# Later ranks of a mixture-of-experts layer get a PSUM bank of their own, and queued sums move to later blocks

## The chip, the cores and the metric

The kernel runs on one core of one Trainium2 chip. The metric is the time of one execution on the device in microseconds (us); the number shown for a kernel is the median of its runs.

## What is computed

Three parts follow one another. Pooled attention (8 batches, 8 heads, 576 positions, head size 64; keys and values averaged over groups of 8) gives 4608 tokens of width 512. Two mixture-of-experts layers follow, each with 8 experts and one expert per token:

```python
    logits = x @ w_gate + modality_bias[modality_id]
    e_idx = np.argmax(logits, axis=1)
...
        h = np.maximum(x[mask] @ w1[e], 0.0)
        out[mask] = gate_w[mask, None] * (h @ w2[e])
```

The second layer has no bias, and it computes only tokens with `x @ w_skip > 0`; a token it skips passes through, and a token it computes is added to its result:

```python
    do_compute = skip_score > 0
    out = x.copy()
    xc = x[do_compute]
...
    out[do_compute] = xc + y
```

The weights are `w1` (8 x 512 x 1024) and `w2` (8 x 1024 x 512), all in fp32.

## The kernel before, in words

Tokens are sorted by expert into blocks of 256. Every fp32 product is made of three products of a high and a low half (`xh`, `xl`, `w1h`, `w1l` and so on). Layer 1 has 18 static blocks, numbered 0 to 17 here, and `body1(i, end)` emits block i:

- **gemm1**: eight steps f, each 12 matmuls of 128x256. Two steps share a PSUM bank (tag "g1", three banks); after the second of a pair ACT writes `hh` (L1474) and DVE `hl` (L1475). Pair 3 (f = 6, 7) reuses the bank of pair 0.
- **gemm2(i, 0)**: 24 matmuls of 128x512, three for each of eight places f. The dictionary `at` hangs work on places. At f = 2 and 4 `next_x` transposes the next block's rows on PE into PSUM (tag "tp", two banks); ACT writes `xh` (L1420) and DVE `xl` (L1423) from there.
- **gemm2(i, 1)**: the other 128 rows, 24 matmuls.

While block i is multiplied, the second layer's routing is made for block i - 1's rows. For each block a queue `todo` holds 18 sums (`logit`, L1800, on DVE), then the two halves of `picks`: `first` (POOL L1731 to L1741, with `rt_mx` on DVE, L1738) and `second` (`rt_my` on DVE, L1747; then POOL `M` L1750, `carry` L1752, `rti` L1753, and the scatter of rows). `drip(n)` takes from the queue until n sums or picks are done. `rank(i)` is two small matmuls on PE (L1779, L1780) into the bank `R2`, a chain of five operations on DVE up to `BB` (L1784 to L1788), and on POOL `RH` (L1789) and four one-hot matrices `OB` (L915). So the chain of one block's routing is: 18 sums, `rt_mx`, POOL's `first` up to `rt_eq`, `rt_my`, POOL's `M`, `carry`, `rti`, then PE's rank, `BB`, `OB`. Each engine works in the order in which its instructions are written.

`arms` holds for blocks 6 to 13, `armed` for blocks 7 to 14. In armed blocks DVE splits the weights of a new expert if there is one, in place of sums; what stayed in the queue is made up in gemm2. Armed blocks rank at place 6 of gemm2(i, 0), the others inside gemm1 after f = 4 and 6:

```python
            if f in (4, 6) and ranks and not armed:
                m.rank(ranks.pop(0))
...
            at = {0: m.drip, 5: pick, 6: partial(m.rank_all, ranks)}
...
            m.drip(8 if armed else 7)
```

In block 16 the second layer's blocks begin to be planned ahead: `start2` has ACT cast the carries (`rc_cb`, L932), and PE sums them over partitions (L936) after f = 1 of gemm1 into the bank of tag "m" (one bank). In block 17 (`late`) the first rows of layer 2 are gathered (POOL L1336, DVE `gi` L1637). After gemm2(17, 0) the head of the queue is taken out as `second`, three sums are dripped, block 18's rows are transposed, and then what was taken out is done:

```python
            _, _, second = m.todo.pop(0)
            m.drip(3)
            next_x(0)
            next_x(1)
            second()
```

Of the kernel before, what the change touches and what calls it, by code (L numbers as in the profile page):

```python
# [9 lines left out]
F32 = mybir.dt.float32  # L10
# [14 lines left out]
E = 8  # L25
# [804 lines left out]
def route(tc, g, r, lg, mask, c0, n, sp, pp, eng, wait=1, then=(), lag=(0, 0)):  # L830
# [52 lines left out]
    for _ in range(4 if wait else 1):  # L883
        yield
    R = pp.tile([128, n, E], F32, tag="m", name="R")
    nc.tensor.matmul(R, lhsT=g.trim, rhs=M, start=True, stop=False)
    nc.tensor.matmul(R, lhsT=g.ones, rhs=I, start=False, stop=True)
    g.bg.hold = True
# [5 lines left out]
    B = r.BB[:, c0:c0 + n]  # L894
    V.tensor_tensor(rk, M, R, ALU.mult)
    yield
# [12 lines left out]
def route_places(tc, g, r, c0, n, eng, eng2=None):  # L909
    for c in range(c0, c0 + n):  # L910
        for i in range(2):
            if c > c0:
                yield
            e = eng2 if eng2 is not None and i else eng
            e.tensor_scalar(g.ob(c)[:, i, :], g.iota, r.BB[:, c:c + 1],  # L915
                            r.pay[:, i, c:c + 1], ALU.is_equal, ALU.mult)
        yield
# [10 lines left out]
def count(tc, g, r, sp, pp, wait, copy=False, cb=None):  # L928
    nc = tc.nc
    if cb is None:  # L930
        cb = sp.tile([128, E], BF16, tag="rc_cb", name="rc_cb", bufs=1)
        (nc.scalar.copy if copy else nc.vector.tensor_copy)(cb, r.carry)  # L932
        for _ in range(wait):
            yield
    N = pp.tile([128, E], F32, tag="m", name="R")
    nc.tensor.matmul(N, lhsT=g.ones, rhs=cb, start=True, stop=True)  # L936
# [256 lines left out]
class Moe:  # L1193
# [575 lines left out]
            in_=self.x2[i % 2][:, t, 0:DM], in_offset=None, bounds_check=NT - 1,  # L1769
            oob_is_err=False)  # L1770

    def rank(self, i):

        nc, g, r2 = self.nc, self.g, self.g.r2
        V = nc.vector
        M, I = r2.M[:, 2 * i:2 * i + 2, :], self.rti[i % 2]
        B = r2.BB[:, 2 * i:2 * i + 2]
        R = self.ps_t("R2")[:, 0, 0:2 * E].rearrange("p (c e) -> p c e", e=E)
        nc.tensor.matmul(R, lhsT=g.trim, rhs=M, start=True, stop=False)  # L1779
        nc.tensor.matmul(R, lhsT=g.ones, rhs=I, start=False, stop=True)  # L1780
        rk = self.sp.tile([128, 2, E], F32, tag="rt_rk", name="rt_rk")
        ra = self.sp.tile([128, 2], F32, tag="rt_ra", name="rt_ra")
        ri = self.sp.tile([128, 2], I32, tag="rt_ri", name="rt_ri")
        V.tensor_tensor(rk, M, R, ALU.mult)  # L1784
        V.tensor_reduce(out=ra, in_=rk, axis=AX.X, op=ALU.add)
        V.tensor_copy(ri, ra)
        V.tensor_scalar(ri, ri, 127, None, ALU.bitwise_and)
        V.tensor_copy(B, ri)  # L1788
        nc.gpsimd.tensor_tensor(r2.RH[:, 2 * i:2 * i + 2], ra, B, ALU.subtract)  # L1789
        for _ in route_places(self.tc, g, r2, 2 * i, 2, nc.gpsimd):  # L1790
            pass

    def rank_all(self, ranks=None):
        ranks = self.ranks if ranks is None else ranks
        while ranks:
            self.rank(ranks.pop(0))

    def logit(self, i, t, e):

# [29 lines left out]
class Layer:  # L1829
# [28 lines left out]
    def second(self):  # L1858

        m, g = self.m, self.m.g  # L1860
        bg = g.bg
        for f in range(8):
            m.gemm1(1, f)
            bg.tick()
            bg.tick()
        m.gemm2(1, 0, self.epilogue)
        bg.flush()
        self.gather(2)
        self.gather(3)
        self.load_regs(2)  # L1870
        self.load_w1(2)
        self.load_w2(2)
        m.load_split(2)
        m.split_w1_if(range(8))
        m.drip(7)
        m.gemm2(1, 1, self.epilogue, {3: lambda: m.xT(2, 0, m.ps_t("ps_x")),
                                      5: lambda: m.xT(2, 1, m.ps_t("ps_x")),
                                      6: lambda: m.gates1(2, m.sp)})
        m.gates2(2, m.sp)
        m.drip(5)  # L1880
# [85 lines left out]
    def body1(self, i, end):  # L1966

        m = self.m
        late = i == self.n_static - 1
        arms = self.ARMS <= i < self.n_static - 4  # L1970
        armed = self.ARMS <= i - 1 < self.n_static - 4
        ranks = m.ranks
        m.ranks = []
        for f in range(8):
            m.gemm1(i, f)
            if f in (1, 3):
                if armed:
                    m.sums_or_w2(f)
                else:
                    m.split_w2_if(range(2 * f - 2, 2 * f + 2))  # L1980
            m.drip(((0, 0, 1, 0, 1, 0, 1, 1) if armed else
                    (0, 0, 1, 1, 1, 1, 2, 2) if late else (1, 1, 1, 2, 1, 2, 1, 1))[f])
            m.g.bg.tick()
            if f in (4, 6) and ranks and not armed:
                m.rank(ranks.pop(0))
            if f == 5 and i == self.n_static - 2:
                m.places2()
            if f == 6 and late:
                m.gather2(i + 1)
                m.load_w1_parts(2, m.e2, end, range(4))  # L1990
        if not armed:
            m.rank_all(ranks)
        m.g.bg.flush()
        m.g.bg.pace = 2
        full = self.load_full(i)
        more = i + 1 < NBLK or end is not None
        if i + 1 < NBLK:
            self.load_w2(i + 1)
        if end is not None:
            m.load_w2_parts(2, m.e2, end)  # L2000

        def next_x(t):
            if t == 0 and end is not None:
                m.gates1(i + 1, m.sp)
            m.xT(i + 1, t, m.ps_t("ps_x"))
            if t == 1:
                m.gates2(i + 1, m.sp)

        if armed:
            new = m.load_split_dve(i)  # L2010

            def pick():
                m.settle_sums()
                m.sums_left(new)
                m.drip()

        if more:
            m.load_split(i + 1)
            if end is None:
                m.gates1(i + 1, m.sp)  # L2020
            m.split_w1_if(range(4))
        if armed:
            at = {0: m.drip, 5: pick, 6: partial(m.rank_all, ranks)}
        elif end is None:
            at = {f: m.drip for f in ((0, 1, 5, 6) if i > 8 else (0, 1, 3, 5, 6))}
        elif late:
            at = {f: m.drip for f in (0, 1, 3, 5)}
        else:
            n = sum(x[1] for x in m.todo) - 2
            at = {f: partial(m.drip, (n + j) // 5) for j, f in enumerate((0, 1, 3, 5, 6))}  # L2030
            at[7] = m.drip
        if more and not late:
            at.update({2: lambda: next_x(0), 4: lambda: next_x(1)})
        m.gemm2(i, 0, self.epilogue, at)
        if late:
# [5 lines that stand above are left out]
        if arms:  # L2041
            m.sums_or_w1(i, range(4, 8))
        elif more:
            m.split_w1_if(range(4, 8))
        if arms:
            pass
        elif end is None:
            m.drip(8 if armed else 7)
        elif not late:
            m.drip()  # L2050
        with m.tc.If(full > 0):
            m.gemm2(i, 1, self.epilogue)
# [126 lines left out]
```

## Time and profile before

| what | us |
|---|---|
| median of 3 runs (lowest, highest) | 932.89 (929.35, 934.34) |
| the profiled execution's own time | 931.96 |
| its span in the profile | 929.9 |
| PE busy | 887.1 (95%) |
| DVE busy | 706.9 (76%) |
| POOL busy | 505.9 (54%) |
| ACT busy | 370.7 (40%) |

The profile is one execution of the program. PE is TensorE, PEld its weight loads, DVE VectorE, ACT ScalarE, POOL GpSimd, SP the engine that issues most DMAs. A row of a timeline gives the start in us from the span's start, the duration, the engine, the source line, the operation with output and inputs, and in brackets how long the engine was idle before and which instruction ended that. Times of all rows are on the clock of the execution before. PEclk is the share of full clock that TensorE was granted.

### The profile page before, as it was taken

Reading aid. Unit: us, or ns where it says so; the run is one execution under the profiler, and the core shown is the slowest. Engines: PE = TensorE matmul, PEld = TensorE weight load, DVE = VectorE, ACT = ScalarE, POOL = GpSimd, SP = SyncE. Lnnn points to the kernel's source line nnn. Section 1 sums busy time; section 2 is a strip of 40 time slices with the busy share of each in tenths; the row PEclk is TensorE's granted clock in tenths of the full one; section 3 lists DMA queues with packets and bytes.
Section 4 is the critical chain, followed back from the end, with each engine's and each line's share of the span. In section 5 each row is a group of like instructions: output and inputs, shape, how many; then the busy total and the mean of one; then the engine's idle time right before and its main releaser. Section 6 shows DMA issues by size and latency. Waiting matters only on the chain. (4 is left out here: it accounts for less than half of the span.)

```text
span 929.9 us, 19087 instructions
## 1 busy us (share of the span) xinstructions
PE 887.1 (95%) x6233; PEld 797.1 (86%) x6233; DVE 706.9 (76%) x1828; ACT 370.7 (40%) x738; POOL 505.9 (54%) x758
## 2 busy tenths in 40 slices
PE   8999999889999999999999978999999999999995
PEld 6899889879899999988888867899888988979983
DVE  5687888877778888789877888877666778687772
ACT  4666556552222222252222511213314566565551
POOL 5796783322346656575766657575652444445441
PEclk9999999999999999999999998999999999999997
DMA  9999954423311221612225321236215772761441
GB/s 233 241 285 294 274 154 147 164 82 111 97 59 65 71 66 40 222 65 68 87 82 185 120 79 65 76 104 227 70 61 166 218 257 88 222 221 36 134 142 44
DMA packets 85950, 126.08 MB, mean 136 GB/s; under 512 B 13000, under 2 KB 49912, under 8 KB 85674
## 3 DMA queue, kind: packets, MB, share of 16 engines
q1 hardware_dynamic: 75194, 96.68, 34.0%
q0 software_dynamic: 10608, 27.67, 9.9%
q8 instruction: 63, 1.03, 0.5%
q14 instruction: 85, 0.70, 0.2%
HBM read 182.09 MB, written 39.50 MB: 238 GB/s over the span
## 5 line engine op out<-in xcount | busy, mean ns | idle before, releaser
L1470 PE MATMUL ps_g<-xh,w1h 128*128 128x256 f32 x896 | 256.8, 287 | 2.2 <-DVE o L1709 1.3
L1470 PE MATMUL ps_g<-xl,w1h 128*128 128x256 f32 x896 | 253.8, 283 | 0.7 <-DVE xl L1423 0.7
L1470 PE MATMUL ps_g<-xh,w1l 128*128 128x256 f32 x896 | 252.8, 282 | 0.0
L1800 DVE CUSTOM_DVE_ANT_0 hr<-x,W 128x512 bf16<-128x512 f32 x324 | 227.8, 703 | 15.7 <-DVEq L1399 4.9
L1519 PE MATMUL ps_g<-w2h,hh 128*128 128x512 f32 x464 | 190.2, 410 | 3.2 <-ACT w2h L1410 1.9
L1519 PE MATMUL ps_g<-w2h,hl 128*128 128x512 f32 x464 | 184.3, 397 | 1.0 <-DVE hl L1475 1.0
L1519 PE MATMUL ps_g<-w2l,hh 128*128 128x512 f32 x464 | 183.5, 395 | 0.0
L1470 PEld LDWEIGHTS ps_g<-xh,w1h 128*128 128x128 f32 x896 | 170.0, 190 | 7.1 <-issue 4.2
L1470 PEld LDWEIGHTS ps_g<-xl,w1h 128*128 128x128 f32 x896 | 169.9, 190 | 2.2 <-DVE xl L1423 1.3
L1470 PEld LDWEIGHTS ps_g<-xh,w1l 128*128 128x128 f32 x896 | 170.3, 190 | 0.0
L1474 ACT ACTIVATE hh<-ps_g 128x512 fp32r<-128x512 f32 (+1 forms) x116 | 67.7, 584 | 244.3 <-PE ps_g L1470 242.2
L1475 DVE SCALAR_TENSOR_TENSOR hl<-ps_g,hh 128x512 fp32r<-128x512 f32 (+1 forms) x116 | 77.7, 670 | 67.3 <-ACT hh L1474 48.3
L1519 PEld LDWEIGHTS ps_g<-w2h,hl 128*128 128x128 f32 x464 | 87.5, 189 | 23.0 <-DVE hl L1475 1.4
L1519 PEld LDWEIGHTS ps_g<-w2h,hh 128*128 128x128 f32 x464 | 87.8, 189 | 21.8 <-issue 2.9
L1519 PEld LDWEIGHTS ps_g<-w2l,hh 128*128 128x128 f32 x464 | 87.9, 189 | 16.1
L915 POOL TENSOR_SCALAR OB<-iota,BB,pay 128x128 bf16<-128x128 bf16 x90 | 86.3, 966 | 12.6 <-DVE BB L903 12.6
L1411 DVE TENSOR_TENSOR w2l<-w2r,w2h 128x512 fp32r<-128x512 f32 x112 | 75.7, 713 | 7.2 <-ACT w2h L1410 4.6
L1346 POOL TENSOR_TENSOR w1l<-w1r,w1h 128x512 fp32r<-128x512 f32 x35 | 45.3, 1315 | 57.7 <-ACT w1h L1343 57.4
L1766 POOL DMA_INDIRECT out_dram<-x,dsi x38 | 46.0, 1210 | 52.6 <-ACT w1h L1343 13.3
L1579 ACT ACTIVATE x<-ps_g,gate 128x512 f32<-128x512 f32 x37 | 25.5, 690 | 103.5 <-PE ps_g L1519 98.6
L1410 ACT CAST w2h<-w2r 128x512 fp32r<-128x512 f32 x112 | 63.9, 617 | 0.1
L1343 ACT CAST w1h<-w1r 128x512 fp32r<-128x512 f32 x112 | 63.7, 619 | 0.4 <-ACT hh L1474 0.4
(303 smaller groups left out, 1437.0 us busy)
## 6 DMA issues: line engine op xcount, KB each, us to landing
w1r<-in_moe_w_dram SPq DMA_DIRECT2D x128, 512.0 KB
w2r<-in_moe_w_dram SPq DMA_DIRECT2D x124, 512.0 KB
x2s<-x SPq DMA_DIRECT2D x19, 522.0 KB
v<-in_v_dram SPq DMA_DIRECT2D x48, 192.0 KB
xd<-x SPq DMA_DIRECT2D x16, 520.0 KB
q_sb<-in_q_dram SPq DMA_DIRECT2D x16, 512.0 KB
kt<-in_k_dram SPq DMA_DIRECT2D x36, 192.0 KB
x2s<-OBx SPq DMA_DIRECT2D x16, 261.0 KB
```

The source lines that it names most:

```text
L915: e.tensor_scalar(g.ob(c)[:, i, :], g.iota, r.BB[:, c:c + 1], r.pay[:, i, c:c + 1], ALU.is_equal, ALU.mult)
L1343: self.nc.scalar.copy(self.w1h[f], raw)
L1346: low() if late is None else late.append(low)
L1410: self.nc.scalar.copy(self.w2h[f], raw)
L1411: (eng or self.nc.vector).tensor_tensor(self.w2l[f], raw, self.w2h[f].bitcast(F32), ALU.subtract)
L1470: nc.tensor.matmul(out, lhsT=a[f][:, k, :], rhs=b[:, k, :], start=(n == 0), stop=(n == 11))
L1474: nc.scalar.activation(out=hh, in_=whole, func=ACTF.Relu)
L1475: nc.vector.scalar_tensor_tensor(hl, in0=whole, scalar=0.0, in1=hh.bitcast(F32), op0=ALU.max, op1=ALU.subtract)
L1519: nc.tensor.matmul(ps, lhsT=a[f][:, tt], rhs=b[f], start=(n == 0), stop=(n == 23))
L1579: nc.scalar.activation(out=self.x2[i % 2][:, t, 0:DM], in_=ps, func=ACTF.Copy, scale=self.gate[i % 2][:, t:t + 1])
L1766: self.nc.gpsimd.indirect_dma_start(out=self.out, out_offset=bass.IndirectOffsetOnAxis(ap=self.dsi[i % 2][:, t:t + 1], axis=0), in_=self.x ...
L1800: self.nc.vector.tensor_tensor_reduce(out=self.junk, in0=self.x2[i % 2][:, t, 0:DM], in1=self.W9[:, e, :], scale=1.0, scalar=0.0, op0=ALU. ...
```

## The change

`rank` takes an argument `own`. With it the two matmuls write a bank of tag "m" instead of one of "tp". Armed blocks (7 to 14) rank at the same place as before with it. A new condition `behind` (blocks 7 to 15) keeps block 15 from ranking inside gemm1 too; it ranks at place 7 of gemm2(15, 0), also in the own bank, and its other places drip. The last drip of a block, after gemm2(i, 0), takes 4 sums in block 14 (8 before), 8 in block 15 and 10 in block 16 (7 before).

```diff
@@ -1769,13 +1769,16 @@
             in_=self.x2[i % 2][:, t, 0:DM], in_offset=None, bounds_check=NT - 1,
             oob_is_err=False)
 
-    def rank(self, i):
+    def rank(self, i, own=False):
 
         nc, g, r2 = self.nc, self.g, self.g.r2
         V = nc.vector
         M, I = r2.M[:, 2 * i:2 * i + 2, :], self.rti[i % 2]
         B = r2.BB[:, 2 * i:2 * i + 2]
-        R = self.ps_t("R2")[:, 0, 0:2 * E].rearrange("p (c e) -> p c e", e=E)
+        if own:
+            R = self.pp.tile([128, 2, E], F32, tag="m", name="R2")
+        else:
+            R = self.ps_t("R2")[:, 0, 0:2 * E].rearrange("p (c e) -> p c e", e=E)
         nc.tensor.matmul(R, lhsT=g.trim, rhs=M, start=True, stop=False)
         nc.tensor.matmul(R, lhsT=g.ones, rhs=I, start=False, stop=True)
         rk = self.sp.tile([128, 2, E], F32, tag="rt_rk", name="rt_rk")
@@ -1790,10 +1793,10 @@
         for _ in route_places(self.tc, g, r2, 2 * i, 2, nc.gpsimd):
             pass
 
-    def rank_all(self, ranks=None):
+    def rank_all(self, ranks=None, own=False):
         ranks = self.ranks if ranks is None else ranks
         while ranks:
-            self.rank(ranks.pop(0))
+            self.rank(ranks.pop(0), own)
 
     def logit(self, i, t, e):
 
@@ -1969,6 +1972,7 @@
         late = i == self.n_static - 1
         arms = self.ARMS <= i < self.n_static - 4
         armed = self.ARMS <= i - 1 < self.n_static - 4
+        behind = self.ARMS <= i - 1 < self.n_static - 3
         ranks = m.ranks
         m.ranks = []
         for f in range(8):
@@ -1981,14 +1985,14 @@
             m.drip(((0, 0, 1, 0, 1, 0, 1, 1) if armed else
                     (0, 0, 1, 1, 1, 1, 2, 2) if late else (1, 1, 1, 2, 1, 2, 1, 1))[f])
             m.g.bg.tick()
-            if f in (4, 6) and ranks and not armed:
+            if f in (4, 6) and ranks and not behind:
                 m.rank(ranks.pop(0))
             if f == 5 and i == self.n_static - 2:
                 m.places2()
             if f == 6 and late:
                 m.gather2(i + 1)
                 m.load_w1_parts(2, m.e2, end, range(4))
-        if not armed:
+        if not behind:
             m.rank_all(ranks)
         m.g.bg.flush()
         m.g.bg.pace = 2
@@ -2020,7 +2024,10 @@
                 m.gates1(i + 1, m.sp)
             m.split_w1_if(range(4))
         if armed:
-            at = {0: m.drip, 5: pick, 6: partial(m.rank_all, ranks)}
+            at = {0: m.drip, 5: pick, 6: lambda: m.rank_all(ranks, True)}
+        elif behind:
+            at = {f: m.drip for f in (0, 1, 5, 6)}
+            at[7] = lambda: m.rank_all(ranks, True)
         elif end is None:
             at = {f: m.drip for f in ((0, 1, 5, 6) if i > 8 else (0, 1, 3, 5, 6))}
         elif late:
@@ -2045,7 +2052,7 @@
         if arms:
             pass
         elif end is None:
-            m.drip(8 if armed else 7)
+            m.drip({14: 4, 15: 8, 16: 10}.get(i - self.n_static + 18, 7))
         elif not late:
             m.drip()
         with m.tc.If(full > 0):
```

PE, block 15. Before, the two matmuls of rank(13) stand inside gemm1, between two matmuls into `ps_g` of `xh`, `xl` and `w1`:

```order
L1470 MATMUL ps_g_8315<-xh_2142,w1l_2575 128x256
L1779 LDWEIGHTS trim
L1779 MATMUL R_8329<-M_673,trim 128x16
L1780 LDWEIGHTS ones
L1780 MATMUL R_8329<-rti_3053,ones 128x16
L1470 MATMUL ps_g_8315<-xh_2142,w1h_2574 128x256
```

Now they stand behind the last matmul of gemm2(15, 0), and those of gemm2(15, 1) follow:

```order
L1519 MATMUL ps_g_8409<-w2h_3043,hl_2577 128x512
L1782 LDWEIGHTS trim
L1782 MATMUL R_8455<-M_673,trim 128x16
L1783 LDWEIGHTS ones
L1783 MATMUL R_8455<-rti_3053,ones 128x16
L1399 UNCONDITIONAL_BRANCH
L2058 COMPARE_AND_BRANCH
L1519 MATMUL ps_g_8517<-w2h_2582,hh_2150 128x512
```

The rank has moved by the rest of gemm1 and all of gemm2(15, 0).

POOL, end of block 15, before: `RH` and `OB` of rank(13) stand ahead of `first` of block 14 (up to `rt_eq` with `desc`), and the scatter and gathers ahead of them.

```order
L1766 DMA out_dram<-x_3050,dsi_3052 4608x512 x2
L1336 DMA xg_2777<-xd,gidx_647 128x520 x2
L1404 UNCONDITIONAL_BRANCH x2
L1789 TENSOR_TENSOR RH_674<-rt_ra,BB_675 128x2
L915 TENSOR_SCALAR OB<-iota,BB_675,pay_677 128x128 x4
L1399 UNCONDITIONAL_BRANCH
L1731 COPY x_3046<-lg_3047 128x2x9
...
L1741 TENSOR_TENSOR rt_eq<-rt_eq,desc 128x16
L1748 TENSOR_TENSOR rt_eq<-rt_eq,rt_my 128x16
```

Now:

```order
L1766 DMA out_dram<-x_3050,dsi_3052 4608x512
L1336 DMA xg_2777<-xd,gidx_647 128x520 x2
L1404 UNCONDITIONAL_BRANCH
L1766 DMA out_dram<-x_3050,dsi_3052 4608x512
L1404 UNCONDITIONAL_BRANCH
L1399 UNCONDITIONAL_BRANCH x2
L2058 UNCONDITIONAL_BRANCH
L1792 TENSOR_TENSOR RH_674<-rt_ra,BB_675 128x2
L915 TENSOR_SCALAR OB<-iota,BB_675,pay_677 128x128 x4
L1731 COPY x_3046<-lg_3047 128x2x9
...
L1741 TENSOR_TENSOR rt_eq<-rt_eq,desc 128x16
L1748 TENSOR_TENSOR rt_eq<-rt_eq,rt_my 128x16
```

On POOL the order of `OB` and `first` is the same; `RH` and `OB` now depend on a rank that PE does later, and one scatter has moved behind the gathers.

DVE, end of block 17. Before (`lg` with `W` are sums, the second row of each reads its result; `xl` is that of block 18):

```order
L1738 TENSOR_REDUCE rt_mx<-lg_3047 128x2
L1800 ISA hr,lg_3051<-x_3050,W_3054 128x512
L1800 ISA lg_3051 128x1
...
L1440 TENSOR_REDUCE g_mx<-xg_2141 128x2
L1441 TENSOR_TENSOR gd_3061<-xg_2141,g_mx 128x2x8
L1423 TENSOR_TENSOR xl_2143<-ps_x,xh_2142 128x4x128 x2
L1453 TENSOR_REDUCE g_su<-gd_3061 128x2
L1454 RECIPROCAL gate_2144<-g_su 128x2
L1747 TENSOR_REDUCE rt_my<-rt_eq 128x2
```

Now:

```order
L1738 TENSOR_REDUCE rt_mx<-lg_3047 128x2
L1747 TENSOR_REDUCE rt_my<-rt_eq 128x2
L1803 ISA hr,lg_3051<-x_3050,W_3054 128x512
L1803 ISA lg_3051 128x1
...
L1440 TENSOR_REDUCE g_mx<-xg_2141 128x2
L1441 TENSOR_TENSOR gd_3061<-xg_2141,g_mx 128x2x8
L1423 TENSOR_TENSOR xl_2143<-ps_x,xh_2142 128x4x128 x2
L1453 TENSOR_REDUCE g_su<-gd_3061 128x2
L1454 RECIPROCAL gate_2144<-g_su 128x2
L1803 ISA hr,lg_3051<-x_3050,W_3054 128x512
```

`rt_my` of block 16 has moved from behind the gates of block 18 to a place ahead of three sums, `g_mx`, `gd` and both `xl`; behind the gates there is a sum instead.

## Rows read from the trace of the kernel before

**Rows 1.** The page, part 1: busy us (share of the span) x instructions

```profile
PE 887.1 (95%) x6233; PEld 797.1 (86%) x6233; DVE 706.9 (76%) x1828; ACT 370.7 (40%) x738; POOL 505.9 (54%) x758
```

**Rows 2.** Table by block: stretch, us, busy us of each engine, granted TensorE clock (PEclk), DMA

```profile
381.94:406.89 24.95, 23.79 (x156) 21.20 (x154) 20.18 (x56) 9.14 (x17) 14.69 (x26) 1.00 0.67 224
...
477.77:501.38 23.61, 23.61 (x156) 21.21 (x155) 18.06 (x54) 5.17 (x9) 14.37 (x27) 1.00 0.21 73
...
521.05:548.10 27.05, 24.32 (x154) 21.26 (x155) 25.44 (x66) 11.17 (x21) 17.00 (x27) 1.00 0.26 87
548.10:579.05 30.95, 26.00 (x156) 23.60 (x154) 25.21 (x77) 5.17 (x9) 22.54 (x47) 0.89 0.19 66
...
602.75:628.21 25.46, 25.46 (x216) 23.09 (x214) 19.14 (x62) 4.95 (x9) 18.88 (x29) 1.00 0.28 95
```

**Rows 3.** Waits, 375 to 640 us: us in total, times, longest

```profile
PE R L1779 <- DVE xl L1423: 3.9, 3, 1.6
```

**Rows 4.** Timeline of PE: start, us, instruction [idle before <- releaser]

```profile
541.70 0.18 PE L1779 MATMUL R<-M,trim 128*128 128x16 bf16 x1 [1.57 <-DVE xl L1423]
...
558.99 0.17 PE L1779 MATMUL R<-M,trim 128*128 128x16 bf16 x1 [3.62 <-POOL M L1750]
560.50 0.17 PE L1780 MATMUL R<-rti,ones 128*128 128x16 bf16 x1 [1.34 <-POOL rti L1753]
...
560.88 0.42 PE L1470 MATMUL ps_g<-xl,w1h 128*128 128x256 f32 x1
...
565.15 0.36 PE L1470 MATMUL ps_g<-xh,w1h 128*128 128x256 f32 x1
565.35 0.28 PE L1470 MATMUL ps_g<-xl,w1h 128*128 128x256 f32 x1
...
566.91 0.28 PE L1470 MATMUL ps_g<-xh,w1l 128*128 128x256 f32 x1
...
581.89 0.18 PE L936 MATMUL R<-rc_cb,ones 128*128 128x8 bf16 x1
```

**Rows 5.** Timeline of DVE, blocks 15 and 16

```profile
557.44 0.69 DVE L1800 CUSTOM_DVE_ANT_0 hr<-x,W 128x512 bf16<-128x512 f32 x1
...
558.18 0.69 DVE L1800 CUSTOM_DVE_ANT_0 hr<-x,W 128x512 bf16<-128x512 f32 x1
...
559.53 0.69 DVE L1475 SCALAR_TENSOR_TENSOR hl<-ps_g,hh 128x512 fp32r<-128x512 f32 x1
...
573.08 0.17 DVE L1454 RECIPROCAL gate<-g_su 128x2 f32<-128x2 f32 x1
575.14 0.17 DVE L1747 TENSOR_REDUCE rt_my<-rt_eq 128x2 f32<-128x16 f32 x1 [1.89 <-POOL rt_eq L1741]
```

**Rows 6.** Timeline of POOL, end of block 15

```profile
568.70 0.20 POOL L1789 TENSOR_TENSOR RH<-rt_ra,BB 128x2 f32<-128x2 f32 x1
...
572.47 0.19 POOL L1731 COPY x<-lg 128x18 f32<-128x18 f32 x1
...
574.88 0.22 POOL L1741 TENSOR_TENSOR rt_eq<-rt_eq,desc 128x16 f32<-128x16 f32 x1
...
578.53 0.66 POOL L1752 TENSOR_TENSOR carry<-carry,M 128x8 f32<-128x8 f32 x1
```

**Rows 7.** Timeline of ACT, block 16

```profile
579.84 0.19 ACT L932 CAST rc_cb<-carry 128x8 bf16<-128x8 f32 x1
```

**Rows 8.** Timelines of POOL, DVE and PE, block 17

```profile
614.24 0.19 POOL L1789 TENSOR_TENSOR RH<-rt_ra,BB 128x2 f32<-128x2 f32 x1 [0.46 <-DVE BB L1788]
...
619.46 1.01 POOL L1336 DMA_INDIRECT xg<-x2s,gi  x1 [0.31 <-issue]
...
626.71 0.22 POOL L1741 TENSOR_TENSOR rt_eq<-rt_eq,desc 128x16 f32<-128x16 f32 x1
...
625.91 1.29 DVE L1423 TENSOR_TENSOR xl<-ps_x,xh 128x512 fp32r<-128x512 f32 x2 [0.76 <-ACT xh L1420]
...
621.77 1.03 PE L1417 MATMUL ps_x<-ident,xg 128*128 128x128 f32 x8
```
## The prediction

> **What bounds the kernel now.** I read the page's busy times first: PE works 95% of the span (its weight loads, PEld, lie beside that) and every other engine at most 76% [rows 1]. A change can therefore gain only the idle time of PE, and it loses wherever it makes PE wait. The second view is a table by block, each stretch from one first matmul of layer 1 to the next. An undisturbed block takes 23.61 us with PE busy throughout [rows 2]. Block 8 takes 24.95 (1.3 more), block 14 27.05, block 15 30.95 at a mean clock of 0.89, and block 17 25.46 without idle time, since it computes more. So about 12 us stand above the undisturbed rate, 7.3 of them in block 15.
>
> The waits and PE's timeline name the causes. The rank's first matmul waits three times for DVE's xl, 3.9 us in all [rows 3]; the one of block 14 is 1.57 at 541.70 [rows 4]. There the rank takes a bank of the two-buffer tag "tp" that the transposed inputs of the next block still hold until DVE has written xl. In block 15 the rank sits inside gemm1: its first matmul waits 3.62 for POOL's M, its second 1.34 for POOL's rti [rows 4]. Behind that, 20 matmuls come at 0.2135 us each (560.88 to 565.15), and later 13 at 0.12 (565.35 to 566.91): half clock, 1.2 instead of 2.4 GHz, worth 20 x 0.0935 = 1.9 us.
>
> **Part 1: the own bank (blocks 7 to 14).** Only the semaphore changes: the rank waits for the last reader of "m" instead of xl. In block 14 the stall of 1.57 goes, so block 15 begins at 548.10 - 1.6 = 546.5. The 1.3 of block 8 goes as well. The third wait (block 13: 3.9 less the 1.57 and some 1.2 of block 8, about 1.1) brings nothing by my reckoning, because the next gemm1 needs the same xl and then DVE's hl, both late there: price 0, with a gain of 1.1 as the other end.
>
> **Part 2: rank(13) leaves gemm1 of block 15.** The 3.62 + 1.34 + 1.9 go. What is late next is hl(15,0), which the third pair of gemm1 waits for, with 4 sums fewer ahead of it. It started at 559.53 [rows 5]; 4 sums at 0.74 (557.44 to 558.18, rows 5) earlier is 556.6, done at about 557.3. PE reaches that place at 546.5 + 6 x 12 x 0.119 = 555.0 (0.12 a matmul, rows 4), so 2.4 of new wait are left. Block 15 then ends 23.6 + 2.4 - 0.15 after 546.5: block 16 begins at about 572.4, 6.6 earlier than now.
>
> **Part 3: what PE meets in block 16.** The count of the carries (L936) sits behind the second f of gemm1, 24 matmuls or 2.85 us into the block, so PE is there at 575.3 (before: 581.89, without a wait, rows 4). It needs rc_cb, a cast on ACT, which needs the carry that POOL writes in second(14). In the new order that chain is later, not earlier:
> - DVE. In block 15 it has no gap to give. Now it ends the gates at 573.08 + 0.17 = 573.25 [rows 5], after 18 sums, four hl, rank(13), rt_mx(14) and two xl. The new order needs 17 sums, four hl, two xl, the gates and rank(13) until BB(13): one sum (0.74) and rt_mx (0.1) less. BB(13) is ready at 572.4.
> - POOL. RH(13) and the four one-hots now stand ahead of first(14), in the stream order. They take 568.70 to 572.47 = 3.77, first(14) takes 572.47 to 575.10 = 2.63 [rows 6]. So rt_eq(14) is ready at 572.4 + 3.8 + 2.6 = 578.8, where it is 575.10 today.
> - second(14): from rt_my at 575.14 [rows 5] to the end of the second carry (578.53 + 0.66 = 579.19, rows 6) are 4.05. That gives carry(14) at 579.0 + 4.05 = 583.1, and the cast of 0.19 [rows 7] and the hand-overs put PE's count at about 583.5.
>
> PE therefore waits 575.3 to 583.5 = 8.2 us and restarts 1.6 later than today: everything that parts 1 and 2 won in blocks 14 to 16 is given back, and 1.6 more. Behind today's wait of 5 us (in two pieces) PE ran at half clock for 1.9 us' worth. For the new wait, longer and in one piece, I take the same 1.9, its nearest row (bounds 0 and 3.8, twice that). Block 17 starts 1.6 + 1.9 = 3.5 later.
>
> The Trainium skill, "TensorE: Matmul & The Clock Gate", Part 1 (the HAM clock gate), says that activity is what releases the throttle and that an idle array falls to 1.2 GHz. The rows of block 15 agree (0.2135 against 0.12 behind the wait); by that rule the 8.2 us of the count's wait would also be followed by half clock, without it the sum would be 1.9 lower.
>
> **Part 4: the end of block 17.** The last drips are 10 sums in block 16 in place of 7. With them the queue is further on when block 17 pops its head as "second": the order shows rt_my(16) on DVE ahead of three sums, g_mx, gd and both xl of block 18, and a logit in the place that rt_my had. rt_my waits for POOL's rt_eq(16), and in the stream POOL does RH(15), four one-hots, four gathers and first(16) before it: 614.24 to 626.93 = 12.7 us, with gaps of 0.3 at most between them [rows 8]. RH(15) at 614.24 comes 3.5 later with PE: 617.7. rt_eq(16) is then ready at about 630.4, 631 if the extra sums ahead of BB(15) delay it too. Behind it on DVE stand 3 sums (2.2), g_mx and gd (0.4), the cast xh on ACT and two xl (625.91 now, 1.29 for both, rows 8): xl ends at 635 to 636.5. PE has the first gathered rows later as well: the second gather ended at 620.47 and PE's transposes ran at 621.77 [rows 8], a margin of 1.3. Gathers and PE move by the same 3.5, unless rank(15) and so the gathers come later still by the extra sums, two of them (1.5), plus a longer stretch of one-hots; for that I take 0.8 (0 to 1.5). Without the xl, gemm1 of block 18 would start at 628.2 + 3.5 + 0.8 = 632.5. With it, at about 636.0, so 3.5 more (bounds 0 and 5.4, the latter with the 1.9 of half clock behind it).
>
> Nothing else changes what PE does: the 18 sums of each block are only moved (0 us as long as DVE has room beyond block 18; if that cover goes, 4 x 0.74 = 3 us), and the x2s write on SP that changes place with the row write of the one-hots waits for what it waited for before.
>
> **The sum.** -1.3 (block 8) + 1.6 + 1.9 (blocks 14 to 16) + 0.8 + 3.5 (block 17) = +6.5. The profiled execution took 931.96, 0.9 under the median of the runs shown (932.89): 938.5 against the profile, 939.0 with half of that 0.9.
>
> **The rivals.**
> - *Only the gain is eaten.* The count waits as forecast, but xl of block 18 is not late (bound 0): -1.3 + 1.6 + 1.9 + 0.8 = +3.0, so 935.0; with no half clock +1.1, 933.1. For it: POOL's spans are rough, and the whole price of 3.5 hangs on one wait. Against: rt_my stands ahead of xl on an engine that works in order.
> - *Faster.* The stalls go and no wait takes their place. Block 16 then begins 6.6 earlier, with block 8's 1.3: -7.9, so 924.5; with block 17's 4.3 still to pay 928.8. The deciding place is PE's count in block 16: it decides below carry(14) at 575.3, and the chain above gives 583.1. Even with carry(14) where it is today (579.2), the count would be at 579.6, only 2.3 earlier than now, and the total -3.6. For it: the stalls are real idle time of the busiest engine. Against: DVE's 17 sums, with no gap to take out. The Trainium skill, "Perfetto Trace Analysis", Optimization Strategy, says that a repeating gap on the engine that should be saturated can mean too few PSUM buffers; by that rule the extra bank is the cure and this rival holds. The trace agrees only for the three waits on xl (3.9 us); the 3.62 and 1.34 end on POOL, which no bank shortens.
> - *The own bank does nothing*: the rank would wait as long for M or rti on POOL. Against: all three waits are put down to xl, not to POOL [rows 3]. Block 8 would keep its 1.3, while the 1.57 of block 14 is eaten at the count either way: 939.0 + 1.3 = 940.3.
>
> **Numbers.** Measurements of this kernel tell a difference from about 0.5% (4.7 us). Forecast 0.60, eaten gain 0.24, faster 0.10, dead bank 0.06. For 8 times in 10: 932.0 (the eaten gain with the clock and the gathers free is 932.3) to 944.0 (939.0 with half clock behind block 18's wait too, 1.9, the longer half clock behind the count, 1.9, and the gathers at their bound, 0.7, is 943.5). Slower by over 0.5% lies above 937.6: most of the forecast and the dead bank, 0.60. Within 0.5%: the eaten gain, the forecast's lower edge and a part of the faster case that keeps carry(14) where it is, 0.31. Faster: 0.09.
>
> **What the profile after would show.** Right: no rank row on PE that waits for xl; no wait inside gemm1 of block 15 but a short one for hl; L936 waiting some 8 us for ACT's rc_cb, with matmuls at 0.21 behind it; rt_my of block 17 idle some 7 us on DVE for rt_eq, and gemm1 of block 18 waiting for xl by 3 to 4 us. Wrong: L936 without a wait (then the time falls below 930), or POOL's first(14) done before 575.

## The result, and the profile after

The changed kernel takes 938.84 us in the median of 14 runs, the kernel before 933.32 beside it (14 runs): a ratio of 1.0061, interval 1.0044 to 1.0078, so slower by 0.6%. The profiled execution took 938.80 (span 936.7), 6.8 more than that of before.

The page's busy times are those of [rows 1] to within 0.3%, and its numbers of instructions are the same: no work was added, only idle time.

```profile
PE 886.7 (95%) x6233; PEld 795.3 (85%) x6233; DVE 705.4 (75%) x1828; ACT 370.0 (39%) x738; POOL 504.7 (54%) x758
```

The table by block, as in [rows 2] (stretch, us, busy us of PE, PEld, DVE, ACT, POOL, granted clock, DMA share, GB/s); the rows are blocks 8 and 13 to 18:

```profile
381.70:405.31 23.61, 23.61 (x155) 21.20 (x154) 18.85 (x54) 9.13 (x17) 13.37 (x24) 1.00 0.64 215
500.00:518.36 18.36, 18.21 (x131) 16.54 (x130) 14.02 (x36) 6.48 (x13) 11.41 (x17) 1.00 0.72 248
518.36:545.02 26.66, 24.47 (x155) 21.34 (x156) 25.09 (x66) 11.05 (x21) 17.60 (x27) 1.00 0.28 89
545.02:571.00 25.98, 23.88 (x156) 21.25 (x155) 22.38 (x69) 4.96 (x9) 14.59 (x28) 1.00 0.18 59
571.00:604.51 33.51, 25.97 (x156) 23.60 (x155) 20.86 (x72) 5.22 (x11) 19.20 (x40) 0.85 0.20 69
604.51:633.87 29.36, 26.07 (x215) 22.81 (x213) 19.82 (x63) 4.94 (x9) 22.51 (x37) 1.00 0.26 82
633.87:659.52 25.65, 25.23 (x155) 22.64 (x155) 20.28 (x58) 9.10 (x17) 11.23 (x13) 0.93 0.61 205
```

Block 8 takes 23.61 where it took 24.95: the 1.3 are gone. Block 13 takes 18.36 (19.67 before), block 14 26.66 (27.05), block 15 25.98 (30.95), at full clock. From block 8 up to the start of block 16 the change has won 1.34 - 0.20 (block 10: 23.86 for 23.66) + 1.31 + 0.39 + 4.97 = 7.8 us. Block 16 takes 33.51 (23.70) and gives all of it back and 2.0 more; blocks 17 and 18 add 3.90 (29.36 for 25.46) and 2.06 (25.65 for 23.59). In the stretch behind them, where layer 2 begins, 1.75 come back (30.05 for 31.80).

The waits of blocks 8 to 18 (engine, line, waited for: us in all, times, longest) have no row of the rank (now L1782) on PE for xl left [rows 3]. The two that matter, on DVE and on PE:

```profile
DVE rt_my L1747 <- POOL rt_eq L1741: 19.8, 7, 7.6
...
PE R L936 <- ACT rc_cb L932: 7.5, 1, 7.5
```

PE's timeline has the places, against [rows 4]:

```profile
555.83 0.39 PE L1470 MATMUL ps_g<-xh,w1h 128*128 128x256 f32 x1 [2.10 <-DVEq L1404]
...
581.53 0.17 PE L936 MATMUL R<-rc_cb,ones 128*128 128x8 bf16 x1 [7.54 <-ACT rc_cb L932]
...
581.92 0.41 PE L1470 MATMUL ps_g<-xl,w1h 128*128 128x256 f32 x1
...
586.18 0.34 PE L1470 MATMUL ps_g<-xh,w1h 128*128 128x256 f32 x1
...
633.87 0.42 PE L1470 MATMUL ps_g<-xh,w1h 128*128 128x256 f32 x1 [1.78 <-ACTq L1399]
634.71 0.58 PE L1470 MATMUL ps_g<-xl,w1h 128*128 128x256 f32 x1 [0.41 <-DVE xl L1423]
```

Gemm1 of block 15 waits 2.10 for hl (the row names a branch of DVE's; it stands right behind hl, which is done at 555.78). The count (L936) waits 7.54 in block 16, where it did not wait before. Behind it 20 matmuls come at 0.213 us (581.92 to 586.18), half clock. Gemm1 of block 18 starts with waits of 1.78 and 0.41. The first is put down to a branch (ACTq). It ends when ACT has written the second xh of block 18, at 632.77 + 1.05 = 633.82; ahead of xh on ACT stands `gd` (L1448), which waited 8.23 for DVE's gd:

```profile
632.65 0.22 ACT L1448 ACTIVATE gd<-gd 128x16 f32<-128x16 f32 x1 [8.23 <-DVE gd L1441]
632.77 1.05 ACT L1420 CAST xh<-ps_x 128x512 fp32r<-128x512 f32 x2
```

The second wait ends with the second xl, at 633.37 + 1.29 = 634.66. Both gd and xl stand on DVE behind rt_my(16), as its rows show, against [rows 5] and [rows 8]:

```profile
570.01 0.17 DVE L1791 CAST BB<-rt_ri 128x2 f32<-128x2 int32 x1
...
571.00 0.17 DVE L1738 TENSOR_REDUCE rt_mx<-lg 128x2 f32<-128x16 f32 x1
576.71 0.17 DVE L1747 TENSOR_REDUCE rt_my<-rt_eq 128x2 f32<-128x16 f32 x1 [5.54 <-POOL rt_eq L1741]
...
630.03 0.17 DVE L1747 TENSOR_REDUCE rt_my<-rt_eq 128x2 f32<-128x16 f32 x1 [7.55 <-POOL rt_eq L1741]
...
633.37 1.29 DVE L1423 TENSOR_TENSOR xl<-ps_x,xh 128x512 fp32r<-128x512 f32 x2 [0.76 <-ACT xh L1420]
```

On POOL, against [rows 6]:

```profile
570.27 0.18 POOL L1792 TENSOR_TENSOR RH<-rt_ra,BB 128x2 f32<-128x2 f32 x1 [5.03 <-DVEq L1399]
...
574.05 0.19 POOL L1731 COPY x<-lg 128x18 f32<-128x18 f32 x1
...
576.45 0.22 POOL L1741 TENSOR_TENSOR rt_eq<-rt_eq,desc 128x16 f32<-128x16 f32 x1
...
580.59 0.66 POOL L1752 TENSOR_TENSOR carry<-carry,M 128x8 f32<-128x8 f32 x1
```

And the cast on ACT that the count needs, against [rows 7]:

```profile
581.28 0.20 ACT L932 CAST rc_cb<-carry 128x8 bf16<-128x8 f32 x1 [9.40 <-POOL carry L1752]
```

The chain of block 16's wait can be read off: BB(13) at 570.01 + 0.17, RH at 570.27, the one-hots to 574.05, first(14) to 576.45 + 0.22 = 576.67, rt_my at 576.71 after an idle time of 5.54 on DVE, the last carry at 580.59 + 0.66, the cast at 581.28, the count at 581.53.

### The profile page after: what moved, and what is told of

The parts are those of the page before. It is cut to its first block, busy times and chain, and to the rows that moved or that the text cites. A ratio compares the mean times of both kernels' runs of the same rounds, so it can differ in the third digit from the quotient of the medians.

```text
span 936.7 us, 19096 instructions
## 1 busy us (share of the span) xinstructions
PE 886.7 (95%) x6233; PEld 795.3 (85%) x6233; DVE 705.4 (75%) x1828; ACT 370.0 (39%) x738; POOL 504.7 (54%) x758
```

## The experiments

Times by block are read as above; "blocks 13 to 17" is the time from the first matmul of block 13 to that of block 18: 126.83 us in the kernel before, 133.87 in the change. Each ratio is to the kernel before on the same chip. Blocks are read from one profiled execution of each kernel. These lie up to 4.1 us from the medians, but much of that lies ahead of the blocks compared: block 8 starts at 379.88 to 385.86, while block 9 takes 23.61 or 23.62 in every kernel.

**The own bank alone.** Rank(13) stays inside gemm1 of block 15 and the drips are as before.

```diff
-        behind = self.ARMS <= i - 1 < self.n_static - 3
+        behind = armed
...
-            m.drip({14: 4, 15: 8, 16: 10}.get(i - self.n_static + 18, 7))
+            m.drip(8 if armed else 7)
```

> Own bank for the ranks of blocks 7 to 14 alone; rank(13) stays inside gemm1 of block 15 and all drips are as before. Theory (block 15's wait ends on POOL's M and rti, behind a DVE without gaps): only what moves that DVE chain counts, that is the 1.3 us of block 8; the 1.1 and 1.6 of blocks 13 and 14 come back as a longer wait inside gemm1 of block 15 (3.62 + 1.34 = 5.0 grows to 6.3 to 8). Time 931 to 932.3 (about -1.4). Rival (an extra bank is what PE lacks): -1.3 - 1.3 - 0.4 as the change shows for blocks 8, 13 and 14, and block 15 no longer than 30.95: 929 to 930.5.

Measured: 930.56, ratio 0.9978 (0.9957 to 0.9999). Blocks 8, 13 and 14 take 23.60, 18.36 and 26.64 as in the change. Block 15, from its table row and PE's timeline:

```profile
548.49:581.47 32.98, 26.29 (x155) 23.89 (x154) 27.10 (x83) 5.17 (x9) 22.79 (x48) 0.84 0.19 64
```

```profile
561.12 0.17 PE L1782 MATMUL R<-M,trim 128*128 128x16 bf16 x1 [5.36 <-POOL M L1750]
```

The wait for M has grown from 3.62 to 5.36 and block 15 from 30.95 to 32.98: what blocks 13 and 14 won (1.7) is eaten in block 15. Blocks 13 to 17 take 127.14, no less than in the kernel before. In this layout the bank alone is worth no more than block 8's 1.3. The time (930.56) lies between the two ranges and can't tell them apart; the block table can.

**Bank and place of the rank, drips as before.**

```diff
-            m.drip({14: 4, 15: 8, 16: 10}.get(i - self.n_static + 18, 7))
+            m.drip(8 if armed else 7)
```

> Own bank, and rank(13) behind gemm2(15,0), but all last drips as before (8, 7, 7). Theory: with 8 sums ahead of it hl(15,0) ends at about 559 and gemm1 of block 15 waits some 5 us for it (2.1 in the change), perhaps with half clock behind; but the last sum of block 14, rt_mx(14) and POOL's first(14) come before rank(13) and its one-hots, so carry(14) is ready at about 575.5 (581.3 in the change) and the count in block 16 waits 0 to 1 us. Block 17 begins 3 to 5 us earlier than in the kernel before, and its end is as before: time 928 to 930.5. Rival (the place of rank(13) makes the count late, whatever the drips): the count waits 4 us or more and the time is 933 to 936.

Measured: 928.57, ratio 0.9967 (0.9941 to 0.9993). The rows of blocks 15 and 16, then PE's, then POOL's last carry of block 14:

```profile
544.78:576.48 31.70, 26.51 (x156) 23.84 (x154) 27.13 (x83) 5.17 (x9) 19.72 (x45) 0.89 0.19 66
576.48:600.20 23.72, 23.72 (x157) 21.43 (x155) 18.77 (x64) 5.23 (x11) 15.07 (x27) 1.00 0.21 74
```

```profile
558.68 0.58 PE L1470 MATMUL ps_g<-xh,w1h 128*128 128x256 f32 x1 [5.19 <-DVEq L1404]
...
579.32 0.18 PE L936 MATMUL R<-rc_cb,ones 128*128 128x8 bf16 x1
```

```profile
573.20 0.66 POOL L1752 TENSOR_TENSOR carry<-carry,M 128x8 f32<-128x8 f32 x1
```

Gemm1 of block 15 waits 5.19 for hl with half clock behind it (0.89); the carry is ready at 573.20 + 0.66 and the count runs at 579.32 without a wait. So it is the drips, not the place of rank(13), that make the count late in the change. The time is in the range, but block 17 begins only 2.1 earlier than in the kernel before, counted from the start of block 8, where 3 to 5 were expected: block 15 is no shorter (31.70 for 30.95), and what is won are blocks 8 and 13.

**Block 17's queue set right in the change.** Two drips fewer in gemm2(17, 0), so that the head of the queue is second(16) again:

```diff
-            at = {f: m.drip for f in (0, 1, 3, 5)}
+            at = {f: m.drip for f in (3, 5)}
```

> The change, but gemm2(17,0) drips at two places instead of four, so that the head of the queue at its end is block 16's second again and rt_my(16) stands behind xl of block 18. Theory: blocks up to 16 as in the change (count waits 7.5); the 7.5 us idle time of DVE ahead of rt_my(16) goes, and with it the 2.2 of PE for xl and the 2.1 by which block 18 is longer, of which up to 1.75 may be lost again at the start of layer 2: 934.5 to 937. Rival (block 18 waits for late gathers or the late routing chain, not for the place of rt_my): no less than 938.

Measured: 935.44, ratio 1.0033 (1.0012 to 1.0055). Blocks 16, 17 and 18:

```profile
574.24:606.37 32.13, 26.07 (x157) 23.70 (x155) 20.67 (x69) 5.23 (x11) 17.75 (x39) 0.89 0.20 72
606.37:633.86 27.49, 25.91 (x215) 22.99 (x214) 21.76 (x69) 4.95 (x9) 21.20 (x35) 1.00 0.32 88
633.86:657.49 23.63, 23.63 (x156) 21.34 (x154) 17.80 (x49) 9.10 (x17) 12.93 (x15) 1.00 0.66 223
```

Block 18 is back at 23.63 and block 17 1.9 shorter than in the change: 1.9 + 2.0 = 3.9 less in these two. Blocks 15 and 16 keep their loss: 27.51 + 32.13 = 59.6 together, 59.5 in the change. Of the 2.0 that block 17 still has over 25.46, 1.6 are the late gathers (0.90 and 0.69 in PE's timeline).

**Pick(14) ahead of rank(13).** As the run before, and in block 15:

```diff
-            at[7] = lambda: m.rank_all(ranks, True)
...
-            m.drip({14: 4, 15: 8, 16: 10}.get(i - self.n_static + 18, 7))
+            n = {14: 4, 15: 8, 16: 10}.get(i - self.n_static + 18, 7)
+            if behind and not armed:
+                while m.todo[1][0] < i:
+                    m.drip()
+                    n -= 1
+                _, _, second = m.todo.pop(0)
+                m.drip(3)
+                second()
+                m.rank_all(ranks, True)
+                n -= 4
+            m.drip(n)
```

> As the run on the place of second, and in block 15 pick(14) ahead of rank(13): first(14), three sums of block 15, second(14), then the rank. Theory: POOL no longer does the 3.8 us of one-hots of rank(13) ahead of first(14), so carry(14) is ready at about 577 instead of 581.3, and the count in block 16 waits 3.5 us (7.5 in the change); 4 us less than the run on the place of second, 930.5 to 933, or 2 less again if no half clock follows the shorter wait. Rival (the carry is late because of DVE's sums, the one-hots lie beside them): the count still waits 6 us or more and the time stays within 1.5 us of that run.

Measured: 933.04, ratio 1.0009 (0.9988 to 1.0029). Blocks 16 and 17, and PE:

```profile
575.49:601.70 26.21, 23.86 (x157) 21.49 (x156) 20.29 (x70) 5.22 (x11) 18.68 (x36) 1.00 0.20 70
601.70:633.19 31.49, 28.66 (x215) 25.13 (x214) 21.89 (x69) 5.04 (x9) 23.93 (x41) 0.89 0.31 87
```

```profile
580.84 0.17 PE L936 MATMUL R<-rc_cb,ones 128*128 128x8 bf16 x1 [2.35 <-ACT rc_cb L932]
...
622.62 0.66 PE L1417 MATMUL ps_x<-ident,xg 128*128 128x128 f32 x4 [1.74 <-DMA xg<-x2s,gi]
```

The count's wait falls from 7.54 to 2.35. Counted from the start of block 14, the last carry is done after 580.55 - 521.45 = 59.1 us, in the change after 581.25 - 518.36 = 62.9: 3.8 less, the one-hots' time. The other 1.4 is PE, which comes later by half clock in block 15 (27.42). But block 17 takes 31.49: PE waits 1.74 and 1.08 for the gathered rows of block 18, and half clock follows (0.89). With 8 and 10 sums at the ends of blocks 15 and 16, rt_mx(15) still stands behind xl. POOL's first(15) waits 4.46 for the sums and starts 24.4 us into block 16 (18.9 in the kernel before); the gathers stand behind it on POOL. That this order is what makes them late was not tested by itself. By the ratios the kernel is some 2 us faster than the run before, where 4 were expected.

**The four sums inside gemm2(15, 0).** Bank and place as in the change; the 4 sums that block 14 leaves are done at the first two places of gemm2(15, 0), all else drips as before.

```diff
-            at = {f: m.drip for f in (0, 1, 5, 6)}
+            at = {0: partial(m.drip, 3), 1: partial(m.drip, 3), 5: m.drip, 6: m.drip}
...
-            m.drip({14: 4, 15: 8, 16: 10}.get(i - self.n_static + 18, 7))
+            m.drip({14: 4}.get(i - self.n_static + 18, 7))
```

> Own bank, rank(13) behind gemm2(15,0), 4 sums fewer at the end of block 14 as in the change, but these 4 are done at the first two places of gemm2(15,0), ahead of rt_mx(14), so that all later drips and the order of the picks are as in the kernel before. Theory (PE loses where the sums push rt_mx and rt_my back): gemm1 of block 15 waits 2.1 us for hl (5.2 in the run with the old drips), rt_mx(14) and carry(14) come when they did in that run, and the count waits under 1 us; block 15 takes 26 to 27.6, block 16 23.7 to 24.7, block 17 25.5: 924 to 927. Rival (fewer sums ahead of hl always come back as a wait at the count, since DVE sets both): block 16 takes 27 or more and the time is that of the run with the old drips, 928 to 930.

Measured: 930.56, ratio 0.9969 (0.9951 to 0.9986). A miss: 924 to 927 were expected.

```profile
549.17:576.59 27.42, 25.29 (x156) 22.65 (x154) 22.73 (x72) 5.07 (x9) 16.48 (x39) 0.94 0.22 75
576.59:604.07 27.48, 25.53 (x156) 22.46 (x155) 23.94 (x77) 5.33 (x11) 20.12 (x34) 0.94 0.18 65
```

```profile
560.01 0.58 PE L1470 MATMUL ps_g<-xh,w1h 128*128 128x256 f32 x1 [2.13 <-DVEq L1404]
...
595.91 0.50 PE L1519 MATMUL ps_g<-w2h,hl 128*128 128x512 f32 x1 [1.95 <-DVE hl L1475]
```

The wait for hl in block 15 is 2.13 and the count doesn't wait, as expected. But a new wait of 1.95 for hl stands at the end of gemm2(16, 0), and both are followed by half clock (0.94). Blocks 14 to 16 take 81.54 together, 82.06 with the old drips and 81.70 in the kernel before. The wait has moved by a block. The rival nearly had the time (928 to 930) and had block 16 (27 or more), but not the place of the wait.

**The old bank in that kernel.** Each rank with `own` false.

> As the run with the sums in gemm2(15,0), but every rank uses the old two-buffer bank. Theory: the waits for xl are back in blocks 8 (1.3), 13 and 14 (1.6), and in block 15 the rank at the last place of gemm2(15,0) waits 3 to 5 us for xl of block 16, as DVE is behind there: 4 to 6 us over that run, 928.5 to 932. Rival (the bank is worth only block 8's 1.3, as in the run with the bank alone): 1 to 2 us over that run.

Measured: 931.97, ratio 0.9987 (0.9967 to 1.0007), 1.4 us over the run before. The weight load of rank(13) in block 15:

```profile
569.16 0.10 PEld L1782 LDWEIGHTS <-trim 128*128 128x128 bf16 x1 [4.41 <-DVE xl L1423]
```

It waits 4.41 for xl, as the theory said (PE itself stands idle for 3.98 there), yet the time is that of the rival. Blocks 14 to 17 take 107.01, 107.07 with the bank: this wait, too, only takes the place of others. Block 13 is another matter. Its 1.3 is lost without the bank and not made up later (blocks 13 to 17: 126.69 for 125.43), so in this layout blocks 8 to 17 give the bank 2.3 us (block 8's 1.3, these 1.3, and 0.2 back in block 10). The same blocks give it 0.9 in the run with the bank alone.

**Two sums left instead of four** (places 0 and 1 drip 4 each, block 14 ends with 2).

> As the run with the sums in gemm2(15,0), with 2 sums left at the end of block 14 instead of 4 and 4 each at the first two places. Theory (DVE has no gap until the carry): the wait for hl in gemm1 of block 15 falls from 2.1 to 0.7, and the 1.4 us come back at xl of block 16 and at the count; within 1 us of that run. Rival (the wait for hl is a loss of its own): 1.4 to 3 us less than that run.

Measured: 930.73, ratio 0.9973 (0.9955 to 0.9992).

```profile
547.15:571.45 24.30, 23.89 (x156) 21.25 (x154) 20.96 (x63) 4.96 (x9) 13.84 (x29) 1.00 0.16 53
571.45:602.11 30.66, 26.23 (x156) 22.52 (x155) 25.75 (x87) 5.23 (x11) 22.35 (x44) 0.94 0.23 84
```

Block 15 takes 24.30 with a wait of 0.41 for hl, block 16 30.66; blocks 14 to 16 take 81.59. That is within 1 us of the run with four, as the theory said. Three ways to lay out the same work (this run, four sums, and the old drips), and 81.5 to 82.1 each time; with block 17, 107.0 to 107.5 in these three and without the bank, 107.2 in the kernel before.

**Less work on DVE.** The layout of the run with four sums inside gemm2(15, 0), with eight sums of block 14's rows left out.

```diff
+        l = [(i, True, (lambda: None) if i == 14 and e in (0, 2, 4, 6) else
+              partial(self.logit, i, t, e)) for e in range(E + 1)]
```

> As the run with the sums in gemm2(15,0), but 8 of the 18 sums of block 14's rows are left out (the products of experts 0, 2, 4 and 6 keep older values, so the second layer's routing of these rows is not the reference's and its number of blocks per expert may differ). Theory (from block 13 to 17 it is DVE's own work that sets the time, wherever it is put): 8 x 0.74 = 5.9 us less on DVE, and PE's waits in blocks 15 and 16 (2.1 and 1.95, and the half clock behind each) go: blocks 13 to 17 take 119 to 121.5 us together, 125.4 in that run. Rival (POOL's chain or the half clock by itself sets it): 124 or more.

Measured: 925.88, ratio 0.9924 (0.9895 to 0.9954).

```profile
546.96:571.25 24.29, 23.87 (x155) 21.25 (x154) 17.17 (x57) 5.17 (x9) 16.38 (x40) 1.00 0.25 86
571.25:596.77 25.52, 23.98 (x156) 21.33 (x155) 22.32 (x72) 5.34 (x11) 18.63 (x32) 1.00 0.20 69
```

Blocks 13 to 17 take 120.27 (125.43 with all sums in the same layout): 5.2 less for 8 x 0.74 = 5.9 us of DVE work. So it is the amount of DVE's work that makes PE wait in these layouts. That the two numbers are so near is not shown to be a rule: in blocks 15 and 16, 2.1 of the gain are waits of PE, and 3.0 are half clock that no longer follows them (PE busy 23.87 + 23.98 for 25.29 + 25.53).

**The sums of block 14's rows on PE.** The same layout, all sums made; those of block 14's rows by the transposes and matmuls that the kernel has for its last block.

```diff
+        l = [(i, True, (lambda: None) if i == 14 else partial(self.logit, i, t, e))
...
+        pe = m.late_logits(14) if i == 15 else None
         for f in range(8):
             m.gemm1(i, f)
+            if pe and f in (2, 3, 5):
+                next(pe)
```

> As the run with the sums in gemm2(15,0), but the 18 sums of block 14's rows are made on PE inside gemm1 of block 15, by the transposes and matmuls that the kernel uses for its last block. Theory: DVE is relieved of 18 x 0.74 = 13.3 us and waits for nothing any more in blocks 15 and 16, PE pays 2 x 0.45 + 1.85 = 2.8 us: blocks 13 to 17 take 121 to 122.5 us together, 3 to 4.5 less than in that run, 926 to 928. Rival (PE's extra work inside gemm1 waits for the copies on ACT and for the transposed rows, and eats it): no gain over that run, 929.5 or more.

Measured: 924.21, ratio 0.991 (0.9877 to 0.9943), the fastest of the study and 0.9% under the kernel before.

```profile
546.41:572.71 26.30, 26.30 (x180) 23.87 (x179) 14.70 (x48) 6.23 (x11) 17.91 (x46) 1.00 0.25 88
572.71:596.40 23.69, 23.69 (x156) 21.40 (x155) 19.61 (x65) 5.22 (x11) 14.03 (x26) 1.00 0.20 65
```

PE is busy through both blocks; block 15 pays 2.7 us of extra PE work. Blocks 13 to 17 take 120.46, a little less than the 121 to 122.5 expected.

**The same in the kernel before, and in the change.** The diff above, put into each.

> The kernel before, with the sums of block 14's rows made on PE as in the run before this, and nothing else changed. Theory (relief of DVE counts only where a place is free to use it: rank(13) inside gemm1 of block 15 still waits for M(13), which hangs on sums of block 13): the wait of 5 us inside gemm1 of block 15 stays but for the 2.8 us of PE's own extra work that lie in it; block 15 takes 30 to 31.5 and blocks 13 to 17 together 126 to 127.5, within 1 us of the kernel before. Rival (DVE's work alone was the bound, bank and place of the rank are beside the point): 121 to 123 together, 926 to 928.

Measured: 931.58, ratio 0.9983 (0.9957 to 1.001). Block 15 and its rank:

```profile
548.21:581.35 33.14, 31.18 (x179) 28.77 (x178) 13.59 (x46) 6.23 (x11) 20.57 (x49) 0.85 0.18 64
```

```profile
557.43 0.17 PE L1779 MATMUL R<-M,trim 128*128 128x16 bf16 x1 [1.06 <-POOL M L1750]
558.49 0.17 PE L1780 MATMUL R<-rti,ones 128*128 128x16 bf16 x1 [0.90 <-POOL rti L1753]
```

The rank inside gemm1 waits 1.06 and 0.90 and PE works in what is left of the old wait, but at half clock for much of the block (0.85): it is busy for 31.18 where the run before needs 26.30. The block takes 33.14, more than the 30 to 31.5 expected, and blocks 13 to 17 take 129.05 (126 to 127.5 expected). Relief of DVE is worth nothing that the time shows while the rank stands there.

> The change, with the sums of block 14's rows made on PE as above. Theory: carry(14) still stands behind rank(13), its four one-hots and first(14), so the count in block 16 waits some 3 us (7.5 in the change); the waits at the end of block 17 (gathers, xl behind rt_my) stay, as they hang on the queue's places and not on DVE's load. Blocks 13 to 17 together 126 to 129 (133.9 in the change, 120.5 with the old places), 931 to 934. Rival (with DVE relieved the places no longer matter): 122 or less together, 926 to 928.

Measured: 934.56, ratio 1.0008 (0.9979 to 1.0037). Block 16 and the count:

```profile
569.39:598.98 29.59, 26.25 (x157) 23.88 (x155) 20.62 (x70) 5.23 (x11) 15.25 (x32) 0.88 0.21 78
```

```profile
575.73 0.17 PE L936 MATMUL R<-rc_cb,ones 128*128 128x8 bf16 x1 [3.34 <-ACT rc_cb L932]
```

The count waits 3.34 (3 expected); block 17 takes 29.37 and block 18 25.89, as in the change. Blocks 13 to 17 take 130.25, a little over the range, by half clock (0.88). So the change's drips and places cost 10 us against the same work with the later drips as before (120.46).

## Why the prediction was right

The time (938.84 for 939.0) and the direction were right. Point by point:

- *Part 1.* Block 8's 1.3 came (1.34). Block 13 was priced at 0 and gave 1.31, block 14 at 1.6 and gave 0.39. Together 1.70 for 1.6. Where block 13's gain went is in PE's timeline of the change: gemm1 of block 14 now waits 0.39 for xl (519.11) and 0.83 for hl (528.64), as the price of 0 had assumed.
- *Part 2.* The 3.62, 1.34 and 1.9 went; the wait for hl is 2.10 for 2.4; counted from the start of block 8, block 15's end came 7.8 earlier than before, and 7.9 had been forecast with block 8's 1.3. That full clock followed the 2.10 is luck in its place: in three other kernels a like wait there cost 1.5 of half clock. It would hardly have changed the total: with block 17's queue set right it came, the count then waited 6.06, and blocks 15 and 16 took 59.6 together for 59.5.
- *Part 3.* The wait of the count, 8.2 by forecast, is 7.54. Its links came 1.9 to 2.2 earlier than forecast: BB(13) 570.2 (572.4), rt_eq(14) 576.7 (578.8), carry(14) 581.25 (583.1); 1.4 of that is DVE's earlier start, since block 8's gain moves DVE too (rt_my(13) at 551.82, 553.19 before). The half clock behind the count cost 33.51 - 23.70 - 7.54 = 2.3 for 1.9. That the order of the drips is the cause, and not the rank's new place, the run with the old drips shows; that the one-hots ahead of first(14) are 3.8 of it, the run with pick(14) first. One reading was not right: DVE does have a gap in block 15 ahead of BB(13), 1.64 for POOL's rt_eq(13) at rt_my(13). It is 1.64 to 1.66 in every kernel here, so it didn't touch the forecast, and no run took it away.
- *Part 4.* The mechanism was there: DVE idle 7.55 ahead of rt_my. The sizes were off in both ways. The waits behind rt_my, for xh and xl, were 1.78 + 0.41 = 2.2 for 3.5, and the gathers 0.87 + 0.64 = 1.5 for 0.8. The last xl came when forecast (634.66; 636.0 less block 8's 1.3), so it is PE that was later there (without the wait 633.87 - 1.78 = 632.1, forecast 632.5 - 1.3 = 631.2). Half clock in block 18 (0.93), put into the range and not into the sum, cost the rest of block 18's 2.06, some 1.65, and 0.6 more is busy time of PE in block 17 (26.07 for 25.46), whose cause is open. Blocks 17 and 18 cost 5.96 for 4.3.
- *What the sum had left out, and luck.* By the end of block 18 the change had lost 8.0, 1.5 more than the 6.5 of the sum. Then 1.75 came back at the start of layer 2, where the kernel before has a mean clock of 0.97 and the change 1.00, and +6.2 was left. No run tested this place alone, but the change is hardly the reason: the same stretch took 30.65 with the bank alone, 30.27 with the old drips and 30.00 with the sums on PE in the kernel before, kernels that have the old order there. That the time came so near to 939.0 is in part luck; the direction and the two waits that make it are not.
- *A slip.* The rivals' 935.0, 933.1 and 932.3 are added up from 932.0, the forecast's 939.0 from 932.4. It moves nothing that the argument rests on.

The Trainium skill's rule on consistent bubbles ("Perfetto Trace Analysis", Optimization Strategy) names too few PSUM buffers as a possible cause, and by it the bank could have been the cure. The run with the bank alone shows what it is worth here: the rank's waits for xl all end, and the time falls by 0.2%, about block 8's share. The engine to relieve was the one that wrote xl. The same section's first sentence, that the most-contended engine can change over time, fits better: PE is busy for 95% of the span, but in block 14 of the change DVE is idle for only 0.66 us and in block 15 for 2.7, and PE waits for it.

## What to carry to other kernels

Where an engine has hardly a gap over several blocks, moving its work moves the wait of the busiest engine and need not shorten it: add up the stretch (here 107.0 to 107.5 us for blocks 14 to 17 in four kernels), not the one block. A move can still lengthen it, as the later drips of the change did (115.5). Then take work off that engine, and see that no fixed place in the order waits for it still: here both together, with the bank, gave 0.9%, the relief alone 0.2% (not clear of the noise), and the bank with the new place 0.3%. A queue that is emptied by counts, and whose head is later taken out by position, has to be counted again whenever one of the counts changes.

## What the runs showed of the hardware

Half clock behind a wait of PE was less regular than one row of before suggested. A wait of 2.10 to 2.14 at the same place of block 15 was followed by full clock in the change (25.98, clock 1.00) and by 13 matmuls or so at 0.21 us in three other kernels (27.42 to 27.51, clock 0.94), 1.5 us more. A wait of 2.35 at the count cost nothing behind it (26.21), one of 3.34 cost 29.59 - 23.70 - 3.34 = 2.6, one of 7.54 2.3. The dearest were two short ones, 1.06 and 0.90 at the rank inside gemm1: PE is busy for 31.18 in that block 15 (clock 0.85) and for 26.30 in the one with the same sums and no wait (clock 1.00), 4.9 more. So in this kernel waits of 2.0 to 7.5 us were followed by 0 to 4.9 us of loss by half clock, and a longer wait did not cost more behind it than a shorter. What decides between them was not settled.
